# Where VectorE's copies of K stand in its queue: third unit instead of tenth, in the second to fourth head pair

## The chip, the cores and the metric

The kernel runs on one core of a Trainium2 chip. The metric is the device time of one execution in microseconds (us). Before the change three runs gave 245.93, 244.68 and 245.98 us, median 245.93. The engines are TensorE (PE, its weight loads PEld), VectorE (DVE), ScalarE (ACT), GpSimd (POOL) and SyncE (SP, which issues DMAs).

## The reference

Two stages, 4 batches of 768 tokens, 8 heads of 64 elements. The first is attention that selects chunks of 32 keys: for each query an upper bound of its score with every chunk is taken from the chunk's minimum and maximum of K, the six best chunks are kept (those after the query's own chunk are excluded), and softmax attention runs over the keys in them that are not after the query:

```
ub = sum(maximum(q * k_min, q * k_max), axis=-1)
top_chunks = argsort(where(causal, ub, -1e9))[..., -6:]
scores = where(sel & (pos_q >= pos_k), scale * q @ k.T, -1e9)
attn_out = softmax(scores) @ v
```

The second is a mixture of experts on the 3072 rows of 512 that come out: a dense part `relu(x @ w1_dense) @ w2_dense` for all rows, and for each row one of eight experts, chosen by the largest gate logit and weighted with its softmax probability.

## The kernel before, in words

**Tiling.** The heads are worked off in 16 pairs (4 per batch, number p). Both heads of a pair lie on 128 partitions, 64 each. A pair has 11 units u = 0 to 10 of up to 512 score columns; in each, TensorE makes scores into a PSUM tile (`scores`, L606), ScalarE takes their exponential (L610), and GpSimd zeroes what lies after the query, in three of the 11 units (L612). One unit later TensorE multiplies with V (`av`, L625). Units 0 to 4 are the first head's, 6 to 10 the second's, unit 5 is shared. After the last unit of a head VectorE normalizes its rows (`norm`: reciprocal L634, product L636), which frees one of two PSUM tiles for the next head's product.

**Selection inside the scores.** The score operands are 128 rows deep: 64 rows are K and the negated queries, the other 64 are a fixed table that marks a key's chunk and, on the query side, flags of the chunks that are not kept. The score matmul thus adds a large number to what is to be dropped. `kT` holds K with the table, `rT` the negated queries with the flags, each in three sets, used in turn by the pairs.

**Preparation of a pair**, in pieces that are called between the units of earlier pairs:
- `prep_k`: TensorE turns K (L543), ScalarE copies it to `kp` (L545, which also puts the keys in order), VectorE takes maximum and minimum of each chunk (L548, two of them) and masks them per head into `kb` (L551).
- `prep_kt`: VectorE copies the halves of `kp` into the two score operands `kT` (L555 and L556).
- `prep_q`: TensorE turns Q (L563), ScalarE makes its positive part (L566), VectorE writes the negated queries into the two `rT` (L567 and L568).
- `prep_ub`: TensorE makes the bounds from `qp`, the negated queries and `kb` (L574, L578), VectorE takes the eight largest of each row (L584, ten instructions) and writes flags (L586).
- `prep_s`: TensorE turns the flags (L592), VectorE copies them into `rT` (L594, L595). The scores of that pair need these copies.

During pair p the pieces k, q, kt and ub are made for pair p + 2, and s for pair p + 1. GpSimd casts K and Q of a later pair (L530, L532) after unit 7, and V (L537) at unit 0.

**What sets the order.** Each engine takes its instructions in a fixed order, which is laid out when the kernel is built: the framework's planner goes by program order, dependencies and its own estimate of times, so that an instruction that is ready can stand ahead of one that was written earlier. `issue_after` ties the pieces that run on TensorE and ScalarE behind the scores and exponentials of a unit; it puts no such tie on VectorE's copies. The call order of the pieces (L771 to L810) thus gives VectorE's order between them. Buffers: three PSUM tiles are shared by all pieces, three by the scores, six tiles hold exponentials.

From the fifth pair on pieces of the second stage (turning of rows, gate, dense part) run between the units; in the first four pairs there are none.

Of the kernel before, what the change touches and what calls it, by code (L numbers as in the profile page):

```python
# [17 lines left out]
def kernel(  # L18
# [499 lines left out]
    with (  # L518
# [15 lines left out]
        def cast_v(p):  # L534
            if p >= NP:
                return
            st[p]["cast"] = nc.gpsimd.tensor_copy(v16[p % NB][:, :, :, 0:D], st[p]["v"])  # L537

        def prep_k(p):
            s = st[p]  # L540
            pk = pprep.tile([128, S], HF, name="pk", tag="pp")
            for t in range(NT):
                nc.tensor.transpose(pk[:, t * 128 : (t + 1) * 128], s["k16"][:, t].rearrange("p g d -> p (g d)"), ident)  # L543
            s["kp"] = kp = ahead.tile([128, S], HF, name="kp")
            nc.scalar.copy(kp.rearrange("d (p j) -> d p j", j=NT), pk.rearrange("d (j p) -> d p j", j=NT))  # L545
            ks = ahead.tile([128, 2, NC], HF, name="ks")
            for i, op in enumerate((ALU.max, ALU.min)):
                nc.vector.tensor_reduce(out=ks[:, i], in_=kp.rearrange("d (c w) -> d c w", w=32), op=op,  # L548
                                        axis=mybir.AxisListType.X)
            s["kb"] = kb = ahead.tile([128, 2, 2, NC], HF, name="kb")  # L550
            nc.vector.tensor_tensor(kb, ks.unsqueeze(2).to_broadcast([128, 2, 2, NC]), hmask, ALU.mult)  # L551

        def prep_kt(p):
            kp = st[p]["kp"]
            nc.vector.tensor_copy(kT[p % NB][0][0:64], kp[0:64])  # L555
            nc.vector.tensor_copy(kT[p % NB][1][64:128], kp[64:128])  # L556

        def prep_q(p):
            s = st[p]
            pq = pprep.tile([128, S], HF, name="pq", tag="pp")  # L560
            pqv = pq.rearrange("d (T h j p) -> d T h j p", h=2, j=NJ, p=64)
            for t in range(NT):
                nc.tensor.transpose(pqv[:, t // NJ, :, t % NJ], s["q16"][:, t].rearrange("p g d -> p (g d)"), ident)  # L563
            s["qp"] = qp = ahead.tile([128, S], HF, name="qp")
            r0, r1 = rT[p % NB]
            nc.scalar.activation(qp, pq, AF.Relu)  # L566
            nc.vector.tensor_single_scalar(r0, pq, -1.0, ALU.mult)  # L567
            nc.vector.tensor_single_scalar(r1[64:128], pq[64:128], -1.0, ALU.mult)  # L568

        def prep_ub(p):  # L570

            s = st[p]
            ub = pprep.tile([128, NT, 2, NC], FP, name="ub", tag="pp")
            nc.tensor.matmul(ub.rearrange("p t g c -> p (t g c)"), ident, cbias.rearrange("p t g c -> p (t g c)"),  # L574
                             start=True, stop=False, skip_group_check=True)
            for t in range(NT):
                for n, (src, j) in enumerate(((s["qp"], 0), (s["qp"], 1), (rT[p % NB][0], 1))):
                    s["ub"] = nc.tensor.matmul(ub[:, t].rearrange("p g c -> p (g c)"), src[:, t * 128 : (t + 1) * 128],  # L578
                                     s["kb"][:, j].rearrange("p g c -> p (g c)"),
                                     start=False, stop=(n == 2), skip_group_check=True)  # L580
            m = m8[p % 2]
            for t in range(1, NT):
                for g in range(2):
                    nc.vector.max(out=m[:, t, g], in_=ub[:, t, g, 0 : 4 * t + 4])  # L584
            flags = fl[p % 2].rearrange("p t (g c) -> p t g c", g=2)[:, :, :, 0:NC]
            s["flag"] = nc.vector.tensor_tensor(flags, ub, m[:, :, :, 5:6].to_broadcast([128, NT, 2, NC]), ALU.is_lt)  # L586

        def prep_s(p):
            s = st[p]
            ps = pprep.tile([128, S], HF, name="ps", tag="pp")  # L590
            for t in range(NT):
                nc.tensor.transpose(ps[:, t * 128 : (t + 1) * 128], fl[p % 2][:, t], ident)  # L592
            r0, r1 = rT[p % NB]
            nc.vector.tensor_copy(r0[64:128], ps[64:128])  # L594
            nc.vector.tensor_copy(r1[0:64], ps[0:64])  # L595
# [3 lines left out]
        def scores(p, u):  # L599
            s = st[p]  # L600
            pc = units[u]
            sp = psc.tile([128, 512], FP, name="sp")
            o = 0
            for g, kt, a, z in pc:
                w = (z - a) * 128
                last = nc.tensor.matmul(sp[:, o : o + w], kT[p % NB][g][:, kt * 128 : (kt + 1) * 128],  # L606
                                 rT[p % NB][g][:, a * 128 : z * 128], start=(o == 0), stop=True, skip_group_check=True)
                o += w
            ex = aexp.tile([128, 512], HF, name="ex")
            scored.append((last, nc.scalar.activation(ex[:, 0:o], sp[:, 0:o], AF.Exp, scale=-0.125)))  # L610
            if pc[0][1] == pc[0][2]:
                latest["pool"] = nc.gpsimd.affine_select(out=ex, in_=ex, compare_op=ALU.is_ge, fill=0.0, base=0,  # L612
                                        pattern=[[0, 4], [1, 2], [2, 64]], channel_multiplier=-1)
            s["ex", u] = ex
# [156 lines left out]
        for i, (p, u) in enumerate(seq):  # L771
            n1 = p + 1 if p + 1 < NP else None
            n2 = p + 2 if p + 2 < NP else None
            if i + ahead_n < len(seq):
                scores(*seq[i + ahead_n])

            with tc.issue_after(scored[-1][0].ins), tc.issue_after(scored[-2][1].ins):
                if p == 0:
                    if u == 3:
                        prep_k(n2)  # L780
                    if u == 6:
                        prep_s(n1)
                    if u == 7:
                        prep_q(n2)
                    if u == 10:
                        prep_kt(n2)
                    if u == 10:
                        prep_ub(n2)
                elif p < HP:
                    if u == 1 and n2 is not None:  # L790
                        prep_k(n2)
                    if u == 2 and n1 is not None:
                        prep_s(n1)
                    if u == 3 and n2 is not None:
                        prep_q(n2)
                    if u == 10 and n2 is not None:
                        prep_kt(n2)
                    if u == 10 and n2 is not None:
                        prep_ub(n2)
                else:  # L800
                    if u == 2 and n1 is not None:
                        prep_s(n1)
                    if u == 4 and n2 is not None:
                        prep_k(n2)
                    if u == 5 and n2 is not None:
                        prep_q(n2)
                    if u == 7 and n2 is not None:
                        prep_kt(n2)
                    if u == 10 and n2 is not None:
                        prep_ub(n2)  # L810
                for f in fills.pop(i % (HP * NU) - LAG, ()):
                    f()
            if i >= LAG:
                finish(*seq[i - LAG])
            if u == (6 if p == 0 else 0) and n2 is not None:
                with tc.issue_after(latest["pool"].ins):
                    cast_v(n2)
                load(p + 4, "v")
                if 1 <= p <= 2:
                    load_dense(st[n2]["cast"], p - 1)  # L820
                for _ in range(PER_PAIR.get(p, 0)):
                    load_expert(*wq.pop(0), st[n2]["cast"])
            if u == 0 and p == NP - 2:
                while wq:
                    load_expert(*wq.pop(0), latest["pool"])
            if u == 5 and p in CONSTS:
                with tc.issue_after(latest["pool"].ins):
                    route_consts(CONSTS.index(p))
            if u == 7:
                with tc.issue_after(latest["pool"].ins):  # L830
                    cast_qk(p + 3)
                load(p + 5, "kq")
            if p == NP - 2 and u == 8:
                load_rows()
                load_offs()
            if p == NP - 1 and u == 8:
                own(0)
            if p == NP - 1 and 3 <= u < 3 + FIRST:
                fetch(u - 3)
# [162 lines left out]
```

## Time and profile before

| | |
|---|---|
| profiled execution, its own time | 245.93 us |
| span of its instructions | 244.2 us |
| median of the runs | 245.93 us (244.68 to 245.98) |
| PE busy | 209.5 us (86%), 2771 instructions |
| DVE busy | 175.8 us (72%), 561 |
| ACT busy | 174.3 us (71%), 325 |
| POOL busy | 161.5 us (66%), 213 |
| mean granted TensorE clock | 0.987 |
| span up to 150 us | attention, with the dense part from the fifth pair on |
| 163 to 215 us | experts: PE busy 51.09 of 52 us |

A busy share is a mean over stages. From 18.9 to 51.0 us, in which the second to fourth pair are worked on, DVE is busy 31.19 of 32.1 us, ACT 28.21, PE 26.07 and POOL 23.44. In a timeline each row is the start in us, the duration, the engine, the line, the operation, what it writes and reads, shapes and a count; a bracket gives the idle time before it and what ended it.

### The profile page before, as it was taken

How to read it: one execution, taken by the hardware profiler on the slowest of the kernel's cores; microseconds unless marked ns; L12 is line 12 of the kernel's file. 1: busy time of each engine (PE TensorE's matmuls, PEld its weight loads, DVE VectorE, ACT ScalarE, POOL GpSimd, SP SyncE). 2: the span in 40 equal slices, each digit the busy share in tenths (PEclk: the TensorE clock that was granted, in tenths of full speed). 3: DMA queues.
4: the chain of work that ended last, by engine and by line, in shares of the span. 5: the costliest groups of instructions: out<-in, count | busy, mean ns of one | idle time of the engine just before them, and what ended most of it. 6: DMA issues, size and time to landing. Idle time of an engine off the chain costs nothing. (4 is left out here: it accounts for less than half of the span.)

```text
span 244.2 us, 7889 instructions
## 1 busy us (share of the span) xinstructions
PE 209.5 (86%) x2771; PEld 149.2 (61%) x2771; DVE 175.8 (72%) x561; ACT 174.3 (71%) x325; POOL 161.5 (66%) x213
## 2 busy tenths in 40 slices
PE   0688788798997989997999997989999989999950
PEld 0466465575765667764667764767566657777720
DVE  3889999999989789796888997677732235555510
ACT  4579798888787899596899886844556556666630
POOL 6458784887288767359878828520688647888881
PEclk9999999999999999999999999999999999999995
DMA  6999999899689899999999999356489999988785
GB/s 176 255 248 281 215 253 262 235 203 219 169 138 347 156 298 223 256 198 225 317 169 261 194 178 226 111 154 182 142 268 223 215 279 235 185 152 117 90 117 109
DMA packets 68279, 50.55 MB, mean 207 GB/s; under 512 B 29712, under 2 KB 61328, under 8 KB 68240
## 3 DMA queue, kind: packets, MB, share of 16 engines
q0 software_dynamic: 15232, 19.32, 48.3%
q1 hardware_dynamic: 53008, 30.72, 45.9%
q8 instruction: 23, 0.38, 0.6%
q14 instruction: 16, 0.13, 0.2%
HBM read 41.93 MB, written 18.23 MB: 246 GB/s over the span
## 5 line engine op out<-in xcount | busy, mean ns | idle before, releaser
L610 ACT ACTIVATE ex<-sp 128x512 f16<-128x512 f32 (+1 forms) x176 | 91.7, 607 | 9.8 <-PE sp L606 8.1
L606 PE MATMUL sp<-rT,kT 128*128 128x128 f16 (+3 forms) x384 | 64.5, 261 | 3.9 <-ACT ex L610 1.1
L612 POOL TENSOR_SCALAR_AFFINE_SELECT ex<-ex 128x512 f16<-128x512 f16 x48 | 32.5, 688 | 37.1 <-ACT ex L610 35.1
L901 POOL DMA_INDIRECT out_dram<-yo,xg x27 | 43.9, 1626 | 12.9 <-issue 5.2
L625 PE MATMUL op<-v,ex 128*128 128x65 f16 x672 | 46.1, 194 | 6.7 <-POOL ex L612 3.2
L625 PEld LDWEIGHTS <-ex 128*128 128x128 f16 x672 | 36.4, 98 | 22.8 <-POOL ex L612 7.3
L390 POOL DMA_INDIRECT table<-xbig,slot x24 | 24.3, 1012 | 17.7 <-issue 17.7
L864 DVE COPY exT<-tp 128x512 f16<-128x512 f16 x28 | 11.8, 423 | 32.8 <-PE tp L862 28.6
L606 PEld LDWEIGHTS <-kT 128*128 128x128 f16 x384 | 28.5, 98 | 7.5 <-issue 4.7
L892 PE MATMUL yp<-we,ehT 128*128 x112 | 30.9, 378 | 0.4 <-ACT ys L431 0.2
L871 PEld LDWEIGHTS <-w 128*128 128x128 f16 x432 | 26.4, 98 | 7.8 <-issue 2.2
L871 PE MATMUL hp<-exT,w 128*128 128x128 f16 x432 | 29.2, 219 | 0.6 <-issue 0.6
L410 PE MATMUL hp<-xT,wd 128*128 128x384 f16 x128 | 28.9, 325 | 0.6 <-DVE xT L266 0.6
L899 ACT ACTIVATE yo<-yp,xg 128x512 f32<-128x512 f32 x27 | 18.6, 688 | 14.0 <-PE yp L892 13.5
L548 DVE TENSOR_REDUCE ks<-kp 128x24 f16<-128x768 f16 x28 | 25.4, 946 | 3.6 <-ACT kp L545 3.3
L426 PE MATMUL yp<-wd,hT 128*128 128x512 f16 x96 | 25.9, 378 | 0.3
L874 ACT ACTIVATE ehT<-hp 128x512 f16<-128x512 f32 x28 | 16.7, 598 | 12.2 <-PE hp L871 8.9
L415 ACT ACTIVATE hT<-hp 128x384 f16<-128x384 f32 x30 | 14.9, 498 | 11.0 <-PE hp L410 10.3
L515 DVE COPY w<-we 128x2048 f16 x27 | 18.8, 697 | 0.2 <-DVE exT L864 0.2
L636 DVE TENSOR_TENSOR xbig<-op,rs 128x384 f16<-128x384 f32 x32 | 17.6, 549 | 0.3
L431 ACT COPY ys<-yp 128x512 f32<-128x512 f32 x21 | 12.7, 606 | 6.0 <-PE yp L426 5.9
L892 PEld LDWEIGHTS <-ehT 128*128 128x128 f16 x112 | 10.2, 97 | 10.4 <-issue 3.7
(158 smaller groups left out, 370.6 us busy)
## 6 DMA issues: line engine op xcount, KB each, us to landing
we<-in_moe_w_dram POOLq DMA_DIRECT2D x16, 512.0 KB, 7.2
kf<-in_k_dram SPq DMA_DIRECT2D x32, 192.0 KB
qf<-in_q_dram SPq DMA_DIRECT2D x32, 192.0 KB
vf<-in_v_dram SPq DMA_DIRECT2D x32, 192.0 KB
out_dram<-ys SPq DMA_DIRECT2D x48, 128.0 KB
xg<-table SPq DMA_DIRECT2D x27, 136.0 KB
table<-zt SPq DMA_DIRECT2D x9, 136.0 KB
wd<-in_moe_w_dense_dram POOLq DMA_DIRECT2D x2, 512.0 KB
```

The lines of the kernel that those rows point to most:

```text
L390: sc = nc.gpsimd.indirect_dma_start(out=table, out_offset=bass.IndirectOffsetOnAxis(ap=keep["slot"][:, t : t + 1], axis=0), in_=xbig[b % 2 ...
L410: nc.tensor.matmul(hp, wd[:, ko, j * 128 : (j + 1) * 128], xT[:, ko, g * G * 128 : (g + 1) * G * 128], start=(ko == 0), stop=(ko == NK - 1))
L426: nc.tensor.matmul(yp, hold["h"][:, j, i * 128 : (i + 1) * 128], wd[:, NK + j], start=(j == 0), stop=(j == NK - 1))
L515: nc.vector.tensor_copy(w.rearrange("p j f -> p (j f)"), w1f[:, bass.ds(offs1[i], NK * 512)])
L548: nc.vector.tensor_reduce(out=ks[:, i], in_=kp.rearrange("d (c w) -> d c w", w=32), op=op, axis=mybir.AxisListType.X)
L606: last = nc.tensor.matmul(sp[:, o : o + w], kT[p % NB][g][:, kt * 128 : (kt + 1) * 128], rT[p % NB][g][:, a * 128 : z * 128], start=(o == ...
L610: scored.append((last, nc.scalar.activation(ex[:, 0:o], sp[:, 0:o], AF.Exp, scale=-0.125)))
L612: latest["pool"] = nc.gpsimd.affine_select(out=ex, in_=ex, compare_op=ALU.is_ge, fill=0.0, base=0, pattern=[[0, 4], [1, 2], [2, 64]], chan ...
L625: nc.tensor.matmul(s["op", g][:, t * (D + 1) : (t + 1) * (D + 1)], ex[:, o : o + 128], v16[p % NB][:, g, kt, :], start=first, stop=(last_o ...
L871: nc.tensor.matmul(hp[:, j], s["w1"][:, ko, j * 128 : (j + 1) * 128], s["xT"][:, ko], start=(ko == 0), stop=(ko == NK - 1), skip_group_che ...
L892: nc.tensor.matmul(yp, s["hT"][:, j], w2f[:, bass.ds(offs[i] + j * 512, 512)], start=(j == 0), stop=(j == NK - 1))
L901: sc = nc.gpsimd.indirect_dma_start(out=out, out_offset=to, in_=o, in_offset=None, bounds_check=N - 1, oob_is_err=False, compute_op=ALU.by ...
```

## The change

In pairs p = 1, 2 and 3 the call of `prep_kt` for pair p + 2 moves from unit 10 to unit 3, ahead of `prep_q`. The conditions on `n1` and `n2` go, since in these pairs there always are two pairs to follow. `prep_kt` itself (two copies of 64 x 768 on VectorE) stays as it is, and the first pair and pairs 4 to 15 keep their own places (units 10 and 7).

```
                 elif p < HP:
-                    if u == 1 and n2 is not None:
+                    if u == 1:
                         prep_k(n2)
-                    if u == 2 and n1 is not None:
+                    if u == 2:
                         prep_s(n1)
-                    if u == 3 and n2 is not None:
+                    if u == 3:
+                        prep_kt(n2)
                         prep_q(n2)
-                    if u == 10 and n2 is not None:
-                        prep_kt(n2)
-                    if u == 10 and n2 is not None:
+                    if u == 10:
                         prep_ub(n2)
```

## The prediction

> **What bounds the kernel now.** The change touches one stretch, so I read the busy time by stretches first, then VectorE's (DVE's) own timeline of one period in it, then what the other engines do in that period. Columns of the first view: stretch and length in us, then per engine busy us and instruction count, then clock, DMA share, GB/s.
>
> ```profile
> 34.98:42.99 8.01, 6.33 (x107) 4.65 (x105) 7.78 (x26) 6.84 (x15) 4.28 (x7) 1.00 1.12 257
> ```
>
> One head pair of this stretch takes 8.01 us. VectorE is busy 7.78 us of it, ScalarE (ACT) 6.84, TensorE (PE) 6.33, GpSimd (POOL) 4.28, and the clock is full. VectorE's timeline (start, duration, line, tiles, shapes, count) shows why it is the pace-setter:
>
> ```profile
> 36.81 0.56 DVE L594 COPY rT<-ps 64x768 f16<-64x768 f16 x1
> 37.41 0.21 DVE L551 TENSOR_TENSOR kb<-ks,hmask 128x96 f16<-128x96 f16 x1
> 37.65 0.55 DVE L595 COPY rT<-ps 64x768 f16<-64x768 f16 x1
> 38.12 0.54 DVE L567 TENSOR_SCALAR rT<-pq 128x768 f16<-128x768 f16 x1
> 38.69 0.56 DVE L568 TENSOR_SCALAR rT<-pq 64x768 f16<-64x768 f16 x1
> 39.27 0.20 DVE L634 RECIPROCAL rs<-op 128x6 f32<-128x6 f32 x1
> 39.38 0.85 DVE L555 COPY kT<-kp 64x768 f16<-64x768 f16 x1
> 40.15 0.54 DVE L636 TENSOR_TENSOR xbig<-op,rs 128x384 f16<-128x384 f32 x1
> 40.72 0.36 DVE L556 COPY kT<-kp 64x768 f16<-64x768 f16 x1
> 41.11 0.91 DVE L584 MAX8 m<-ub 128x8 f32<-128x8 f32 x10
> ...
> 42.52 0.55 DVE L636 TENSOR_TENSOR xbig<-op,rs 128x384 f16<-128x384 f32 x1
> 42.99 1.80 DVE L548 TENSOR_REDUCE ks<-kp 128x24 f16<-128x768 f16 x2
> ```
>
> No row carries an idle time: each instruction begins when the one before lets go. One row does not fit: the first K copy, L555, takes 0.85 us, its twin L556, of the same shape, 0.36. Grouped over 18.9 to 51 us (count, then busy us and mean ns, then idle time before) this is the rule, not an accident:
>
> ```profile
> L555 DVE COPY kT<-kp 64x768 f16<-64x768 f16 x4 | 3.3, 820 | 0.0
> ...
> L556 DVE COPY kT<-kp 64x768 f16<-64x768 f16 x4 | 1.4, 357 | 0.1
> ```
>
> GpSimd's timeline of the period names the partner:
>
> ```profile
> 35.63 0.82 POOL L532 CAST q<-qf 128x768 f16<-128x768 f32 x1
> 38.58 0.67 POOL L612 TENSOR_SCALAR_AFFINE_SELECT ex<-ex 128x512 f16<-128x512 f16 x1 [2.13 <-ACT ex L610]
> 39.19 0.83 POOL L537 CAST v<-vf 128x768 f16<-128x768 f32 x1
> ```
>
> The V cast runs from 39.19 to 40.02; L555 starts at 39.38, inside it, and ends at 40.23, 0.21 after it. So L555 stands still for about 0.85 - 0.36 = 0.49 us until the cast is over. L567 and L568, which read PSUM, run beside the causal selection L612 (38.58 to 39.25) at 0.54 and 0.56 and lose nothing.
>
> ScalarE and TensorE follow VectorE, with less room than the busy shares suggest:
>
> ```profile
> 37.91 2.06 ACT L610 ACTIVATE ex<-sp 128x512 f16<-128x512 f32 x4 [1.13 <-PE sp L606]
> 39.84 0.83 ACT L545 COPY kp<-pk 128x768 f16<-128x768 f16 x1
> 40.52 3.04 ACT L610 ACTIVATE ex<-sp 128x384 f16<-128x384 f32 x6
> ...
> 44.30 0.48 ACT L610 ACTIVATE ex<-sp 128x384 f16<-128x384 f32 x1
> 45.92 2.94 ACT L610 ACTIVATE ex<-sp 128x512 f16<-128x512 f32 x6 [1.13 <-PE sp L606]
> ```
>
> ```profile
> 37.43 0.60 PE L606 MATMUL sp<-rT,kT 128*128 128x128 f16 x5 [0.32 <-DVE rT L594]
> ...
> 38.77 0.18 PE L578 MATMUL ub<-kb,rT 128*128 128x48 f16 x1
> ...
> 39.18 0.49 PE L543 MATMUL pk<-ident,k 128*128 128x128 f16 x6
> ...
> 40.74 0.53 PE L625 MATMUL op<-v,ex 128*128 128x65 f16 x12 [0.45 <-DVE xbig L636]
> ```
>
> Per pair ScalarE waits 1.13 us for the first scores, these wait 0.32 us for the flags that VectorE copies (L594), and the value matmuls wait 0.45 us for the normalization L636. All three go back to VectorE's queue.
>
> **The change part by part.** Six copies move, two in each of three pairs; no instruction, DMA or byte is added or removed, and SP's and GpSimd's own lists stay. On VectorE the copies pass the two negations (L567, L568) and the first half's normalization (L634, L636), and now stand behind L595. I take program order there, because before, too, the row order is the order of the units. The copies' input is ready: the kp that ends at 40.67 in the period shown (39.84 + 0.83) is copied in the next period, whose L595 stands at 45.66 (37.65 + 8.01), 5 us later.
>
> From the start of L595 to the start of the maxima, before: 41.11 - 37.65 = 3.46 us. After, each step is the spacing of two neighbouring rows: L595 to its successor 0.47 (38.12 - 37.65); L555 unhindered 0.36 (L556's duration); L556 to its successor 0.39 (41.11 - 40.72); L567 0.57 (38.69 - 38.12); L568 0.58 (39.27 - 38.69); L634 0.20, its own duration, since L636 needs its result and nothing lies between them any more (before, L555 filled 0.11 of it, 39.38 - 39.27); L636 0.47 (42.99 - 42.52). Sum 3.04. **VectorE is 0.42 us shorter per pair, 1.3 us in three.**
>
> Two things decide whether the price 0.36 + 0.36 holds. First, where the copies land against GpSimd. In the period shown L555 would run 38.12 to 38.48 and L556 38.48 to 38.84, and L612 begins at 38.58: the second copy is ahead by 0.10 us. The trace has both outcomes:
>
> ```profile
> 57.48 0.73 DVE L556 COPY kT<-kp 64x768 f16<-64x768 f16 x1
> ...
> 87.04 0.36 DVE L556 COPY kT<-kp 64x768 f16<-64x768 f16 x1
> ```
>
> ```profile
> 57.14 1.59 POOL L612 TENSOR_SCALAR_AFFINE_SELECT ex<-ex 128x512 f16<-128x512 f16 x2 [1.65 <-ACT ex L610]
> ...
> 87.18 0.75 POOL L612 TENSOR_SCALAR_AFFINE_SELECT ex<-ex 128x512 f16<-128x512 f16 x1 [2.52 <-ACT ex L610]
> ```
>
> Where the copy is first (87.04 against 87.18) it keeps 0.36, and L612 takes 0.75, 0.08 more than 0.67. Where L612 is first (57.14 against 57.48) the copy takes 0.73, 0.37 more. Selection and copy both hang on L594, so the 0.10 should be steady: I take 0.36, with 0.73 as the other end. The Trainium skill ("SBUF — State Buffer", section "Who interferes with whom") says that whichever of the two starts first holds the shared port for its whole instruction while the other blocks fully; by that rule L612 would be held until 38.84, 0.26 rather than 0.08, which the rows at 87 us do not show and which would not move the sum, since GpSimd idles 2.13 us before it.
>
> Second, what is late. The negations come 0.75 us later (0.36 + 0.39). The bound's matmuls on the negated queries (L578, 38.77, 0.11 after L567's end at 38.66) are next in TensorE's queue, and K's transposes (39.18) stand behind them. If the planner leaves that order, kp cannot start on ScalarE before 39.18 + 0.75 + 0.49 = 40.42 instead of 39.84: 0.58 later, and six exps with it. The last exp then ends at 44.78 + 0.58 = 45.36. Nothing in the rows shows the next pair's scores ready at once, so I bound their exps by the present distance less the present wait: 45.92 - 44.78 - 0.33, where 0.33 is what the scores wait for L594 (0.32 in the row), gives 0.81 and a start at 46.17, against 45.92 - 0.42 = 45.50 by VectorE alone. In the first period ScalarE thus eats the gain and 0.25 us more. From then on its own loop is the limit: 45.59 - 37.91 = 7.68 us against 8.01, a gain of 0.33 in each following pair. Three pairs: +0.25 - 0.33 - 0.33 = **-0.4 us**. If the planner issues K's transposes ahead of the late matmuls (nothing ties them), kp stays at its place, and ScalarE's loop allows 0.33 a pair, **-1.0 us**; VectorE's full sum is **-1.3**. I take -0.5, nearer to the first, because the order in the trace is the only one shown.
>
> After the stretch I let the shift pass undiminished: the next stage has its waits among the same engines, and I found no fixed time in it. The profiled execution took 245.93 us (span 244.2, 1.73 around it) and equals the median of the runs, so the forecast is 245.93 - 0.5 = **245.4 us**.
>
> **The rivals.**
>
> *A. VectorE's gain passes whole.* For it: VectorE has no idle, ScalarE has 1.13 us per pair. Against it: the late transposes. 245.93 - 1.3 = 244.6 us.
>
> *B. The stall changes its partner.* L612 gets in first and L556 costs 0.73 each time: 0.42 - 0.37 leaves 0.05 a pair, and ScalarE's lateness stays: about +0.3, 246.2 us. The mask L551 could be caught instead, since VectorE moves up against the Q cast (35.63 to 36.45; L551 at 37.41, a distance of 0.96, less 0.42 for each pair gained, less what the cast moves back):
>
> ```profile
> 75.57 1.40 DVE L551 TENSOR_TENSOR kb<-ks,hmask 128x96 f16<-128x96 f16 x1
> ```
>
> ```profile
> 75.47 0.83 POOL L532 CAST q<-qf 128x768 f16<-128x768 f32 x1
> 76.24 0.67 POOL L612 TENSOR_SCALAR_AFFINE_SELECT ex<-ex 128x512 f16<-128x512 f16 x1
> ```
>
> There L551 took 1.40 instead of 0.21, to the end of two GpSimd instructions back to back (76.91). Once at the third pair this costs 1.2 and leaves +0.7 on the forecast's -0.5, so about 246.6. The same section of the Trainium skill says that an instruction with two SBUF inputs contends with a GpSimd instruction that reads SBUF; the row at 75.57 agrees, with 1.40.
>
> *C. Slower.* The place is L556 behind L555. It decides if L556 starts later than L612 (38.58), that is by a loss of 0.10 us in front of it, and then waits as L551 did at 75.57, through L612 and the V cast that follows without a gap, to 40.02 + 0.21 = 40.23 instead of 38.84. That is 1.39 a pair against 0.42 gained: +0.97, in three pairs +2.9, 248.8 us. Against it: the copy at 57.48 got in between two selections (end 58.21, the pair of them ended at 58.73).
>
> *D. The order elsewhere changes.* The order on each engine is laid out ahead, from estimates of time (L594 stands between the reductions and their mask L551, though it comes after both in the program). A copy that moves by seven units may change what the planner does in later pairs. The size of one such wait is a row of VectorE's later stage:
>
> ```profile
> 83.11 1.81 DVE L548 TENSOR_REDUCE ks<-kp 128x24 f16<-128x768 f16 x2 [1.55 <-ACT kp L545]
> ```
>
> One more or one less of 1.55 on top of -0.5 gives 247.0 or 243.9.
>
> *E. The change does not do what it says:* the planner puts the copies where they were, as fillers. The time stays 245.9.
>
> **How the numbers follow.** Within 0.5% (1.23 us) a measurement of this kernel can't be told from no change. Forecast 0.38, of which 0.03 falls beyond that bound on the fast side by scatter. A 0.22: its 244.6 lies 0.1 past the bound, so 0.15 faster and 0.07 same. B 0.12: 0.10 same, 0.02 slower. C 0.11, slower. D 0.13: 0.08 faster, since it starts from a gain, and 0.05 slower with scatter; two such waits would be needed to go much further. E 0.04, same. Sums: faster 0.26, same 0.56, slower 0.18. The range holds A and both ends of D and leaves C out with the outer part of D: 243.8 to 247.3.
>
> **What would show it.** Right: L555 and L556 at 0.36 each ahead of L567 in pairs two to four, no row of 0.8 there, and VectorE's period near 7.6. The step on ScalarE is right if kp (L545) starts some 0.6 later after the first exps, and the wait before the first exps falls from 1.13 to a few tenths or none while VectorE now shows idle time before L594 or L636. A: that wait stays above 0.5 and the fifth pair's first scores come 1.2 us earlier. B and C: a K copy of 0.7 (B) or 1.7 (C) beside L612, or L551 above 1 us. D: the order of TensorE's or VectorE's rows after 51 us differs. Wrong altogether: L567 or L568 longer than 0.56 beside the V cast, which now falls on them.

## The result, and the profile after

The changed kernel takes 247.74 us (median of nine runs, 247.12 to 248.32) against 245.30 us for the kernel before on the same chip (243.07 to 246.71): a ratio of 1.0121, 95% interval 1.0090 to 1.0152. (Here and below the ratio is worked out from the single runs; it lies close to the quotient of the two medians, here 1.0099, but is not the same.) The kernel is slower by 2.4 us, where 0.5 us less had been forecast, and 0.4 us above the range. The profiled execution took 247.46 us with a span of 245.8.

VectorE's timeline of the period that the prediction costed, in the changed kernel:

```profile
36.50 0.56 DVE L594 COPY rT<-ps 64x768 f16<-64x768 f16 x1
...
37.33 0.55 DVE L595 COPY rT<-ps 64x768 f16<-64x768 f16 x1
37.81 0.34 DVE L555 COPY kT<-kp 64x768 f16<-64x768 f16 x1
38.16 0.36 DVE L556 COPY kT<-kp 64x768 f16<-64x768 f16 x1
...
40.49 0.90 DVE L584 MAX8 m<-ub 128x8 f32<-128x8 f32 x10
```

The copies stand where they were put and take 0.34 and 0.36; the 0.85 is gone. The period, from one L594 to the next (36.50 here, 43.97 below), is 7.47 us instead of 8.01. So the second and third pair did become shorter than in the profile before. The loss lies behind them. VectorE in the fourth pair, same kernel:

```profile
43.97 0.56 DVE L594 COPY rT<-ps 64x768 f16<-64x768 f16 x1
44.56 0.78 DVE L551 TENSOR_TENSOR kb<-ks,hmask 128x96 f16<-128x96 f16 x1
...
45.85 0.75 DVE L555 COPY kT<-kp 64x768 f16<-64x768 f16 x1
46.62 0.88 DVE L556 COPY kT<-kp 64x768 f16<-64x768 f16 x1
...
52.18 0.56 DVE L594 COPY rT<-ps 64x768 f16<-64x768 f16 x1
...
62.83 0.56 DVE L594 COPY rT<-ps 64x768 f16<-64x768 f16 x1 [0.74 <-PE ps L592]
...
75.32 0.56 DVE L594 COPY rT<-ps 64x768 f16<-64x768 f16 x1
...
82.83 0.56 DVE L594 COPY rT<-ps 64x768 f16<-64x768 f16 x1
```

L594 comes once per pair, so its starts are a clock of the kernel. In the profile before they fell at 44.82, 51.22, 61.35, 71.64 and 80.44; the first and the last of the five:

```profile
44.82 0.56 DVE L594 COPY rT<-ps 64x768 f16<-64x768 f16 x1
...
80.44 0.56 DVE L594 COPY rT<-ps 64x768 f16<-64x768 f16 x1
```

The changed kernel is 0.85 us ahead at the fourth pair and 2.39 us behind at the eighth. It loses 3.24 us in four intervals: 8.21 instead of 6.40, 10.65 instead of 10.13, 12.49 instead of 10.29, and 7.51 instead of 8.80. Two things can be seen there. In the fourth pair three VectorE instructions take 0.78, 0.75 and 0.88 instead of 0.21, 0.36 and 0.36, together 1.48 us more. And from the fifth pair on TensorE, VectorE and ScalarE do the same work in another order, as the planner laid it out anew; GpSimd's rows stand in the order of before.

GpSimd beside those three rows, changed kernel:

```profile
42.53 0.45 POOL L172 MEMSET xbig<- 128x192 f16 x2
...
43.44 0.81 POOL L530 CAST k<-kf 128x768 f16<-128x768 f32 x1
...
44.46 0.81 POOL L532 CAST q<-qf 128x768 f16<-128x768 f32 x1
45.73 0.67 POOL L612 TENSOR_SCALAR_AFFINE_SELECT ex<-ex 128x512 f16<-128x512 f16 x1 [0.45 <-ACT ex L610]
46.34 0.94 POOL L537 CAST v<-vf 128x768 f16<-128x768 f32 x1
```

In this pair GpSimd writes the routing's constants (L172 to L176, 0.9 us) ahead of the casts of K and Q. The Q cast begins at 44.46, and L551, at 44.56, is 0.10 us too late and stays until 45.34, 0.07 after the cast's end. The first copy then begins at 45.85, inside L612 (45.73 to 46.40), and ends at 46.60; the second begins inside the V cast (to 47.28) and ends at 47.50.

### The profile page after: what moved, and what is told of

It is laid out like the page before. It is cut to its first block, busy times and chain, and to the rows that moved or that the text cites. A ratio compares the mean times of both kernels' runs of the same rounds, so it can differ in the third digit from the quotient of the medians.

```text
span 245.8 us, 7889 instructions
## 1 busy us (share of the span) xinstructions
PE 210.4 (86%) x2771; PEld 149.6 (61%) x2771; DVE 175.3 (71%) x561; ACT 174.2 (71%) x325; POOL 161.6 (66%) x213
## 4 chain that ended last, share of the span: by engine, by line
DVE 28%; PE 27%; DMA 13%; issue 12%; POOL 10%; ACT 5%; POOLq 1%; SPq 1%; DVEq 0%; ACTq 0%
DVE ks L548 7%; DMA out_dram<-yo,xg 6%; PE yp L891 5%; PE hp L870 4%; PE hp L410 4%; DMA xg<-table 4%; POOL table L390 3%; ACT ex L610 3%; DVE m L584 3%; POOL ex L612 3%; PE yp L426 2%; PE sp L606 2%; DVE rT L568 2%; DMA qf<-in_q_dram 2%; DVE xbig L636 2%
## 5 line engine op out<-in xcount | busy, mean ns | idle before, releaser
L606 PE MATMUL sp<-rT,kT 128*128 128x128 f16 (+3 forms) x384 | 63.3, 262 | 4.5 <-DVE rT L594 1.5
L612 POOL TENSOR_SCALAR_AFFINE_SELECT ex<-ex 128x512 f16<-128x512 f16 x48 | 32.3, 683 | 35.9 <-ACT ex L610 34.9
L625 PE MATMUL op<-v,ex 128*128 128x65 f16 x672 | 45.6, 195 | 6.4 <-POOL ex L612 4.1
L636 DVE TENSOR_TENSOR xbig<-op,rs 128x384 f16<-128x384 f32 x32 | 17.6, 551 | 0.5
```

Of the source, the lines that this page charges most:

```text
L625: nc.tensor.matmul(s["op", g][:, t * (D + 1) : (t + 1) * (D + 1)], ex[:, o : o + 128], v16[p % NB][:, g, kt, :], start=first, stop=(last_o ...
L636: nc.vector.tensor_tensor(xbig[b % 2][:, :, h0 : h0 + D], opv[:, :, 0:D], rs.to_broadcast([128, NT, D]), ALU.mult)
```

## The experiments

Two causes were thus to be told apart, which could both be true: **the collisions** in the fourth pair, and **the order** from the fifth pair on. A third question was where the gain of the earlier pairs had gone. In all kernels below the copies are called as before unless the edit says otherwise; nothing of the computation is left out in any.

**Copies moved in the second and third pair only.** From the fifth pair on the order of this kernel is that of the kernel before.

```
-                    if u == 3 and n2 is not None:
-                        prep_q(n2)
-                    if u == 10 and n2 is not None:
+                    if u == 3 and p < 3:
                         prep_kt(n2)
-                    if u == 10 and n2 is not None:
+                    if u == 3: prep_q(n2)
+                    if u == 10:
+                        if not (p < 3): prep_kt(n2)
                         prep_ub(n2)
```

> The copies are moved in the second and third pair only (p = 1 and 2); in the fourth they stay at unit 10, and every engine's order from the fourth pair on is that of the kernel before. If the loss comes from the fourth pair's move (its collisions with GpSimd, and the other order behind it): VectorE's period is near 7.5 us in the two pairs, and the time is 0.3 to 1.0 us below before (ratio 0.996 to 0.999). If the loss comes from the moved copies in every pair alike (about 0.8 us each): 1.6 us above before (1.007).

Measured: 0.9991 (0.9961 to 1.0020), 244.66 us. This kernel isn't free of collisions: in its profile the mask L551 of the fourth pair takes 0.79 us instead of 0.21. **Copies moved in the fourth pair only** (`p == 3` in place of `p < 3`):

> The copies are moved in the fourth pair only (p = 3). VectorE is then not ahead of GpSimd when it gets there. If the loss is the planner's other order from the fifth pair on, it is all here without the collisions: 1.5 to 3 us above before (1.006 to 1.012). If it is VectorE's collisions with GpSimd in the fourth pair, which need the lead from the pairs before: 0 to 0.5 us above (1.000 to 1.002).

Measured: 1.0118 (1.0083 to 1.0154), 247.29 us. The whole loss hangs on the fourth pair's move, and no gain shows from the move in the two pairs before it. VectorE in the kernel with the fourth pair moved alone:

```profile
31.51 0.36 DVE L555 COPY kT<-kp 64x768 f16<-64x768 f16 x1
...
44.01 0.56 DVE L594 COPY rT<-ps 64x768 f16<-64x768 f16 x1
44.61 0.21 DVE L551 TENSOR_TENSOR kb<-ks,hmask 128x96 f16<-128x96 f16 x1
...
45.32 0.39 DVE L555 COPY kT<-kp 64x768 f16<-64x768 f16 x1
45.72 0.36 DVE L556 COPY kT<-kp 64x768 f16<-64x768 f16 x1
...
81.41 0.56 DVE L594 COPY rT<-ps 64x768 f16<-64x768 f16 x1
```

This kernel has no collision in the fourth pair and is as slow as the changed one, so the order alone can cost this much. Its first row holds the other surprise: at the old place, where the profile before had 0.85, the copy takes 0.36 (and 0.31 one period later).

**The kernel before, profiled once more.** That called for a second profile of the unchanged kernel:

> The kernel before in its own order, profiled once more, to see whether the stall of the first K copy on GpSimd's V cast (0.85 instead of 0.36 us) is there in every execution. Always there: L555 at 0.8 to 0.85 in the second to fourth pair. Not always: at 0.3 to 0.4 in some of them, and VectorE's period then near 7.5 us instead of 8.0.

It took 244.68 us with a span of 243.0. Its VectorE rows:

```profile
31.40 0.35 DVE L555 COPY kT<-kp 64x768 f16<-64x768 f16 x1
...
36.39 0.56 DVE L594 COPY rT<-ps 64x768 f16<-64x768 f16 x1
...
38.95 0.31 DVE L555 COPY kT<-kp 64x768 f16<-64x768 f16 x1
...
43.90 0.56 DVE L594 COPY rT<-ps 64x768 f16<-64x768 f16 x1
44.50 0.21 DVE L551 TENSOR_TENSOR kb<-ks,hmask 128x96 f16<-128x96 f16 x1
...
46.47 0.31 DVE L555 COPY kT<-kp 64x768 f16<-64x768 f16 x1
```

The same program, the same place, 0.35, 0.31 and 0.31 instead of 0.85, 0.85 and 0.80, and a period of 7.51 instead of 8.01. The stall that the change was to end is in one profiled execution of this kernel and not in another. Four more kernels here leave the copies of the second and third pair in place. In the third pair the first copy is held up in two of them (the two below that move GpSimd's constants and nothing else: 0.85 and 0.84) and not in the other two (0.31 each): three profiled executions of six have the stall there. GpSimd's rows say what decides, before first, then the second profile:

```profile
31.18 0.83 POOL L537 CAST v<-vf 128x768 f16<-128x768 f32 x1
```

```profile
31.49 0.94 POOL L537 CAST v<-vf 128x768 f16<-128x768 f32 x1
```

In the first the copy began at 31.37, 0.19 behind the cast, and stood until the cast was over. In the second it began at 31.40, 0.09 ahead of the cast, and kept 0.35, while the cast took 0.94, 0.11 more. In the next two periods the copy kept 0.31 and the cast took 0.97 and 1.01; there the starts are 0.02 and 0.01 us apart, too close for the rows to say which came first.

The two executions part in the first pair, at GpSimd's cast of Q, again before first, then the second profile:

```profile
22.04 0.83 POOL L532 CAST q<-qf 128x768 f16<-128x768 f32 x1 [0.38 <-DMA qf<-in_q_dram]
```

```profile
22.41 0.83 POOL L532 CAST q<-qf 128x768 f16<-128x768 f32 x1 [0.81 <-DMA qf<-in_q_dram]
```

It waits for the transfer of its input, 0.38 us in one and 0.81 us in the other. The V cast after it then begins at 23.66 and 24.00, and the first pair's copy, at 23.91 and 23.84, is behind it in the one (0.79) and ahead of it in the other (0.35). That the arrival of this transfer sets the course is read from two traces; no run changes it.

**The order held.** Two kernels separate order and move. The first has the move in all three pairs, but TensorE, VectorE and ScalarE are tied, from the fifth to the ninth pair, to the order that the kernel before has there. The second leaves the copies at their old place and takes the changed kernel's order. The ties are of the kind `NoSync`: they add no waiting on a semaphore and only fix the planner's sequence:

```
+        ORDER = {"PE": [(1,4),(0,1),(4,9), ...
+        made = list(nc.cur_bb.bb.instructions)[edge[(4, 0)]:edge[(9, 0)]]
+        for name, spans in ORDER.items():
...
+            for x, y in zip(line, line[1:]):
+                tc.add_manual_dep(y, x.name, mybir.DependencyInfo(
+                    mybir.DependencyClass.NoSync, mybir.DependencyReason.DATA), reason="order")
```

Copies moved, order of before:

> The changed kernel (copies moved in all three pairs), with the order on TensorE, VectorE and ScalarE held, from the fifth pair on, to the order of the kernel before. If the planner's other order is the cause: the loss is gone, ratio 0.996 to 1.002. If it is the copies' new place itself (their collisions in the fourth pair): the loss stays, 1.008 to 1.015.

Measured: 1.0069 (1.0044 to 1.0094), 247.15 us against 245.31. Copies not moved, order of the changed kernel:

> The opposite: the copies stay at unit 10 in every pair, and the order on TensorE, VectorE and ScalarE from the fifth pair on is held to that of the changed kernel. The order as the cause: the loss is there without the change, ratio 1.008 to 1.014. The copies' place as the cause: 0.998 to 1.002.

Measured: 1.0102 (1.0062 to 1.0142), 247.67 us. VectorE of this second kernel:

```profile
51.38 0.56 DVE L594 COPY rT<-ps 64x768 f16<-64x768 f16 x1
...
62.03 0.56 DVE L594 COPY rT<-ps 64x768 f16<-64x768 f16 x1 [0.74 <-PE ps L592]
...
74.52 0.56 DVE L594 COPY rT<-ps 64x768 f16<-64x768 f16 x1
...
82.03 0.56 DVE L594 COPY rT<-ps 64x768 f16<-64x768 f16 x1
```

No copy moved, and the intervals 10.65, 12.49 and 7.51 are those of the changed kernel. The order alone costs about 1%. The first kernel shows that something else costs too: with the old order it is still 0.7% slower, and its fourth pair has L551 at 0.79, L555 at 0.75 and L556 at 0.88, as in the changed kernel.

**The constants in another pair.** To move the collisions the constants were put into the second pair (`CONSTS = (1, 4, 5)` for `(3, 4, 5)`), once with the change and once, as its control, without:

> All three pairs as in the changed kernel; GpSimd's first routing constants (six short fills) are made in the second pair instead of the fourth, so that its casts of K and Q in the fourth pair begin some 0.9 us earlier and are out of VectorE's way. The order on TensorE, VectorE and ScalarE is that of the changed kernel. Collisions as the cause: L551, L555 and L556 fall from 0.78, 0.75, 0.88 to 0.21, 0.36, 0.36 in the fourth pair, and the time to 1.0 to 1.5 us below the changed kernel (ratio 1.006 to 1.008 to before). The other order as the cause: at most 0.3 us below it (1.011).

> Control for the run before it: the kernel before, with GpSimd's first routing constants made in the second pair instead of the fourth, nothing else. Both theories: within 0.3 us of before (0.999 to 1.001).

Measured: 1.0156 (1.0118 to 1.0194) with the change, 1.0062 (1.0032 to 1.0092) without. The collisions went along. VectorE with the change:

```profile
29.48 1.21 DVE L551 TENSOR_TENSOR kb<-ks,hmask 128x96 f16<-128x96 f16 x1
...
31.20 0.61 DVE L555 COPY kT<-kp 64x768 f16<-64x768 f16 x1
31.82 0.88 DVE L556 COPY kT<-kp 64x768 f16<-64x768 f16 x1
```

They stand in the second pair now, and the fourth has none. In the control L551 takes 1.20 at the same place and the two copies, which are not moved, 0.31 and 0.36; in its next two pairs, though, the first copy takes 0.85. So it is the constants that make GpSimd late, and the moved copies are the second and third to be caught. The control costs 0.6% itself, so this edit shows the mechanism and does not price it.

**The constants behind the casts.** In the fourth pair they are called after the casts of K and Q:

```
-            if u == 5 and p in CONSTS:
+            if u == (8 if p == 3 else 5) and p in CONSTS:
```

Four kernels have this line: with the move and the order of before, with the move alone, with the move in the second and third pair only, and without any move.

> The changed kernel with the order of the kernel before held from the fifth pair on, and GpSimd's first routing constants (six short fills) made behind its casts of K and Q in the fourth pair instead of ahead of them, so that the casts are over some 0.9 us earlier, when VectorE comes to L551. Collisions in the fourth pair as the second cause: L551, L555 and L556 there fall from 0.79, 0.75, 0.88 to 0.21, 0.35, 0.36, and the loss of the run without this (1.0069) is gone: 0.997 to 1.002. Not the cause: 1.005 to 1.009.

> The changed kernel in its own order, with the same constants behind the casts. Both causes at work in the changed kernel: what is left is the order alone, 1.005 to 1.010. The order alone as the cause: 1.010 to 1.014, as the changed kernel. The collisions alone: 0.998 to 1.003.

> The copies moved in the second and third pair only, the fourth as before, with the same constants behind the casts. In the run without this L551 stood 0.79 us in the fourth pair. If such collisions are what is left: 0.21 there, and 0.3 to 0.8 us below before, 0.996 to 0.999.

> Control: the kernel before with the same constants behind the casts, nothing else. VectorE does not meet the casts there before (L551 0.21 to 0.25), so both theories: 0.998 to 1.002.

| kernel | ratio to before | interval |
|---|---|---|
| move, order of before | 0.9980 | 0.9948 to 1.0012 |
| move, its own order | 1.0081 | 1.0048 to 1.0114 |
| move in second and third pair | 0.9976 | 0.9944 to 1.0008 |
| no move | 0.9977 | 0.9945 to 1.0008 |

VectorE of the first of them:

```profile
44.08 0.21 DVE L551 TENSOR_TENSOR kb<-ks,hmask 128x96 f16<-128x96 f16 x1
...
44.79 0.34 DVE L555 COPY kT<-kp 64x768 f16<-64x768 f16 x1
45.15 0.36 DVE L556 COPY kT<-kp 64x768 f16<-64x768 f16 x1
```

No collision, the old order, and no loss: the intervals after the fourth pair are 6.37, 10.14, 10.28 and 8.78 us. The last three are those of the kernel before in both profiles, to within 0.02; the first is that of its first profile (6.40) and not of its second (5.94). This closes the square: collisions alone 1.0069, order alone 1.0055 to 1.0118 (the kernels above and one repetition below), both 1.0121, neither 0.9980. The two do not add up fully; the intervals are too wide to say by how much, but the traces agree: some 1.5 us of standing VectorE instructions lengthen the interval behind the fourth pair by 2.80 us in the old order (9.17 against 6.37) and by 1.51 in the new one (8.21 against 6.70).

The move by itself is worth nothing that these runs resolve: 0.9980 with it in all three pairs, 0.9976 in two (where the fourth pair's first copy, left in place, takes 0.85 us), 0.9977 without. The traces say why. From the second pair's L594 to the fifth's the kernel before takes 22.41 us with the stall (28.81 to 51.22) and 21.00 without it (28.84 to 49.84); the moved one, with neither collision nor new order, takes 21.30 (28.56 to 49.86). So it gains 1.1 us on one course and loses 0.3 on the other. If half of the executions took each course, as three profiles of six do, that would be 0.4 us, an estimate from these rows and 0.16% of the time; the intervals are 0.3% wide to each side. None of these kernels is faster than the one before beyond its interval.

**What in the order costs the time.** The longest wait of VectorE and TensorE that the changed kernel has and the one before has not is in the seventh pair. VectorE, changed kernel:

```profile
72.29 0.46 DVE L586 TENSOR_TENSOR fl<-ub,m 128x288 f16<-128x288 f32 x1
74.52 0.20 DVE L634 RECIPROCAL rs<-op 128x6 f32<-128x6 f32 x1 [1.77 <-PE op L625]
```

TensorE's rows beside it, same kernel:

```profile
74.25 0.30 PE L625 MATMUL op<-v,ex 128*128 128x65 f16 x4 [1.90 <-POOL ex L612]
...
74.55 0.50 PE L592 MATMUL ps<-ident,fl 128*128 128x128 f16 x6
```

The turning of the flags (L592), whose input has been there since 72.75 (72.29 + 0.46), stands behind value matmuls that wait 1.90 us for L612, and VectorE's L594 behind a reciprocal that waits for the same. L612 in turn stands behind scatters, the first of which waited 2.91 us, where the second profile of before has 0.55. GpSimd, changed kernel:

```profile
71.13 1.07 POOL L390 DMA_INDIRECT table<-xbig,slot  x1 [2.91 <-issue]
```

These scatters take their offsets from `slot`, which VectorE writes in L310. Changed kernel first, then the second profile of before:

```profile
70.04 0.19 DVE L310 TENSOR_REDUCE slot<-rt 128x6 int32<-128x48 f32 x1
```

```profile
66.13 0.19 DVE L310 TENSOR_REDUCE slot<-rt 128x6 int32<-128x48 f32 x1
```

In both the first scatter begins 0.90 us after the end of L310 (71.13 after 70.23, 67.22 after 66.32), and in every other profile here 0.89 to 0.91 us after it. So the new order of VectorE, in which L310 ends 7.40 us after the last L594 instead of 6.35, holds GpSimd up by 1.05 us.

In the kernel before the flags are turned ahead of the value matmuls that wait in TensorE's rows above. Five matmuls, these four and the score matmul after them, were put behind the turning, with the rest of the changed kernel's order kept:

> The changed kernel in its own order, but for five matmuls on TensorE in the seventh pair: four value matmuls of unit 5 that wait for GpSimd's selection, and the score matmul after them, stand behind the transposes of the eighth pair's flags and K instead of ahead of them, as in the kernel before. If this wait (1.9 us in the trace of the run with the fourth pair's copies alone) holds up the flags and so the next pair: 1.0 to 1.8 us below the changed kernel, ratio 1.004 to 1.008. If the time goes elsewhere, and the short pair behind it makes up for the wait: at most 0.5 us below, 1.010 to 1.012.

Measured: 1.0099 (1.0059 to 1.0138); the interval between the two L594 stays at 12.48 us, since L594 still stands behind the reciprocal (75.04 after L634 at 74.24). Then both engines' rows were swapped, on the kernel with the constants behind the casts, and that kernel was run again beside it:

> The changed kernel in its own order with the constants behind the casts (1.0081 to before without more), but for two places in the seventh pair, both as in the kernel before: on TensorE the five matmuls of the earlier run stand behind the transposes of the eighth pair's flags and K, and on VectorE the two copies of these flags (L594, L595) stand ahead of a normalization (L634, L636) that waits for the value matmuls, and so for GpSimd. If the flags' way through two queues that stand behind GpSimd's scatter is the cost: the 12.5 us between the flag copies of the seventh and the eighth pair fall to some 10.5, and the time by 0.8 to 1.8 us, ratio 1.001 to 1.005. If the cost is spread over the fifth to seventh pair in other ways: 1.006 to 1.009.

> The kernel it is compared with, on the same chip: the changed kernel with the constants behind the casts, in its own order throughout. Both theories: 1.006 to 1.010, as before.

Measured: 1.0061 (1.0031 to 1.0090) with the swap, 1.0055 (1.0028 to 1.0082) without. VectorE with the swap:

```profile
61.32 0.56 DVE L594 COPY rT<-ps 64x768 f16<-64x768 f16 x1 [0.74 <-PE ps L592]
...
71.85 0.56 DVE L594 COPY rT<-ps 64x768 f16<-64x768 f16 x1 [0.60 <-PE ps L592]
...
80.94 0.56 DVE L594 COPY rT<-ps 64x768 f16<-64x768 f16 x1
```

The interval fell from 12.49 to 10.53, as that theory had it. The next one rose from 7.51 to 9.09, and the time did not move. The longest wait was real, but taking it away did not bring the time back; 1.6 of the 2.0 us turned up in the next pair. Both kernels with this swap or part of it keep the late L310, and with it the scatters' wait of 2.91 us; an edit that puts L310 back was not run. **Which part of the order costs the time stays open.** What is shown is that the order as a whole costs 0.6 to 1.2%. The traces spread that over the intervals: against the second profile of before, the kernel with the fourth pair moved alone loses 0.82 (6.76 against 5.94), 0.51 (10.64 against 10.13) and 2.20 (12.49 against 10.29) and regains 1.26 (7.51 against 8.77), 2.27 us in all; the kernel with the new order and no copy moved loses 2.23 over the same four intervals.

## Why the prediction was wrong

**The stall of 0.49 us, "this is the rule, not an accident".** This step failed first. The four rows it was read from (one of them the first pair's, which is not moved) were one execution, and in one execution the outcome mostly repeats from period to period; it changed only where something else had shifted the engines against each other. The second profile of the same kernel has 0.35, 0.31 and 0.31 there, and from L595 to the maxima 40.19 - 37.22 = 2.97 us, where the step counted 3.46. The new place needs 3.16 there (40.49 - 37.33 in the changed kernel; 3.04 was predicted, and 0.10 of the difference is the second half's reciprocal, which now runs ahead of L636 too). Against an execution without the stall there was nothing to gain. The measured ratios agree: 0.9980 with the move and without its side effects, 0.9977 without the move. An execution with the stall can still profit, by some 1.1 us; how many of the runs of before have it is not known beyond the profiles, three of six.

**The copies keep 0.36, the second ahead of L612 by 0.10.** Right in the second and third pair: 38.16 against L612 at 38.26 in the changed kernel, and 0.34 and 0.36 as durations. Here the selection took 0.78, which is 0.11 longer than 0.67, not the 0.26 of a full block. The Trainium skill ("SBUF — State Buffer", "Who interferes with whom") says that the order of issue decides who blocks; the collisions shown here agree wherever the starts lie 0.06 us or more apart, but the rows of a GpSimd instruction that comes second show only 0.11 to 0.18 us more.

**The negations 0.75 later, K's transposes behind them, kp 0.58 later.** The branch taken was the wrong one. The planner put K's transposes ahead of the late matmuls, which the step had named as the alternative. In the changed kernel's TensorE and ScalarE rows:

```profile
38.46 0.50 PE L543 MATMUL pk<-ident,k 128*128 128x128 f16 x6
...
39.17 0.20 PE L578 MATMUL ub<-kb,rT 128*128 128x48 f16 x1
```

```profile
37.59 2.06 ACT L610 ACTIVATE ex<-sp 128x512 f16<-128x512 f32 x4 [0.47 <-PE sp L606]
39.52 0.83 ACT L545 COPY kp<-pk 128x768 f16<-128x768 f16 x1
```

From the first exps to kp it is 1.93 us, as before (39.84 - 37.91). ScalarE's wait fell from 1.13 to 0.47, and no gain was eaten there. It changed nothing in the outcome.

**"I let the shift pass undiminished".** This is the step with the large error: the sum has no term for the stage behind the stretch, as if its order stayed. Rival D named the mechanism, a new order in later pairs, but priced it as one wait of 1.55 starting from a gain of 0.5, and gave it 0.05 on the slow side. The trace shows 2.27 us, and there was no gain to start from: 245.3 + 2.27 = 247.6 is past the 247.0 it allowed.

**Rival B's mask.** L551 was caught by the Q cast, at half the price (0.57 us more rather than 1.2) and in the fourth pair rather than the third. What the rival left out is that the caught mask pushes both copies into L612 and the V cast, another 0.39 and 0.52. Together the 1.48 us exceed what it allowed. The trigger was a part of the program that the prediction never looked at: the constants that GpSimd writes in this pair. Where the constants stay ahead of the casts and the copies of the second and third pair are moved, L551 starts 0.09 to 0.10 us behind the Q cast (44.56 against 44.46 in the changed kernel). Where the copies are not moved it is ahead by 0.06 to 0.07 if there was no stall (44.50 against 44.56 in the second profile of before), and comes near the cast's end if there was (45.41, with the cast from 44.78 to 45.59, in the first). So the rival's picture, VectorE moving up against the cast, holds against the first profile only; against the second it is GpSimd that moved up, by 0.16 us, and that was enough.

**Rival C** did not come: no copy waited through two GpSimd instructions. **The sum.** At the eighth pair the changed kernel stands 3.80 us behind the second profile of before (82.83 against 79.03): 0.07 from the first four pairs, 2.27 from the order (the figure of the kernel with the fourth pair moved alone) and 1.45 from the collisions (8.21 against its 6.76). 2.8 are left at the end (245.8 against 243.0); the rest is made up later, which the runs do not explain further.

## What to carry to other kernels

A stall that repeats in one profiled execution may be one of two outcomes of a race: profile the same kernel a second time before pricing its removal, above all where two starts lie within 0.2 us of each other. Where a planner lays out each engine's order, a moved call can reorder other stages; compare the orders of both kernels stage by stage, and hold the old one to see what the edit itself is worth. A long new wait is not yet the loss: take it away and see whether the next interval gives it back.

## What was not expected of the hardware

The unchanged kernel has two courses through the same stretch, with a period of 8.01 us or 7.51 us, which differ in whether a VectorE copy begins 0.19 us behind a GpSimd cast or 0.09 us ahead of it (both profiled; spans of 244.2 and 243.0 us). The price of such a meeting is uneven: a VectorE copy that comes second stands still until about 0.2 us after the GpSimd instruction's end (0.36 becomes 0.75 to 0.88), while a GpSimd instruction that comes second is longer by 0.11 to 0.18 us in its row (L612 0.78 for 0.67, the V cast 0.94 to 1.01 for 0.83). Where GpSimd's instructions follow each other without a gap, L551 (0.21 us alone) waited through all of them: with the constants in the second pair and the copies moved it took 1.21 us from 29.48, through K cast (28.75 to 29.61), constant and Q cast (29.77 to 30.62).
